# Linear attention feeding a two-layer MLP: fewer ones columns in the kv matmul, z spread in the mask multiply, one batch's num a slot later

## Chip, cores, metric

One core of one Trainium2 chip. The metric is device microseconds of the whole kernel. The inputs are fp32; the matmuls run in bf16 with fp32 sums.

## The reference, cut to what matters

```python
q_p, k_p = phi(q), phi(k)                          # phi(x) = elu(x) + 1; B=8, H=8, S=576, D=64
kv  = einsum('bhsd,bhse->bhde', k_p, v)
z   = sum(k_p, axis=2)
num = einsum('bhsd,bhde->bhse', q_p, kv)
den = einsum('bhsd,bhd->bhs', q_p, z)[..., None] + 1e-6
x   = (num / den)  ->  4608 tokens x 512
h   = x @ w_in                                     # 512 -> 2048
out = (h - tanh(h)) @ w_out                        # 2048 -> 512
```

## The kernel before

TensorE works through nine chunks of 512 tokens: 64 first-layer matmuls, then 64 of the second layer, each of 512 columns. The attention of the next batch is slipped into numbered slots between them (`s1[fi]` after a first-layer group, `s2[s]` after four second-layer matmuls). A batch has 576 tokens, so batch 2 is needed as chunk 2 starts.

```python
vp = const.tile([128, 2, J, 136], BF16, name="vp")     # J = 9; per row: 128 columns of v, 8 ones
...
def a_vp(b, i):                                         # VectorE copies v into vp
    nc.vector.tensor_copy(vp[:, i, :, 0:128].rearrange("p j (h d) -> p h j d", h=2), v_b[b % 2][:, 0:2, i])

def a_kv_cols(b, banks):                                # batches 2 to 7
    ...
    ps = [banks()[:, 0:272].rearrange("p (i e) -> p i e", i=2) for hg in range(2)]
    for i in range(2):
        for j in range(J):
            for hg in range(2):                         # two 64-row halves of the array: a pair
                r = slice(64 * hg, 64 * hg + 64)
                nc.tensor.matmul(ps[hg][:, i, :], kp[r, i, j].rearrange("p h d -> p (h d)"),
                                 vp[r, i, j, :], start=(j == 0), stop=(j == J - 1))
    for hg in range(2):
        nc.vector.tensor_mul(kz_t[b][:, hg, :, 0:136], ps[hg], mask[:, hg, :, 0:136])
...
# a_den:    four small matmuls per pair of heads with z, then rden = 1 / (den + 1e-6)
# a_spread: rden -> DRAM tile ds -> rdb, broadcast over 64 partitions (two DMA hops)
# a_num:    a 512-column matmul into PSUM bank 6 or 7, then xT = psum * rdb on VectorE
...
nc.gpsimd.memset(vp[:, :, :, 128:136], 1.0)
load_v(1)
load_wo(2)
load_wo(3)
...
    elif n1 < B:                                        # n1 = c + 1
        s1[8 if c == 1 else 5].append(lambda: a_kv_cols(n1, attn))
        s1[10 if c == 1 else 8].append(lambda: (a_den(n1, attn), a_spread(n1)))
        for p in range(NP + 1):                         # NP = 4: five nums
            s2[(11 if c == 1 else 9) + p].append(lambda p=p: a_num(n1, p))
```

The eight ones columns give z eight times over, so that one masked multiply puts z into the eight rows that den reads.

## Time and profile before

| | before |
|---|---|
| time, median of 3 runs | 294.0 us (293.95 to 294.2) |
| span of the profiled run | 291.8 us |
| TensorE / VectorE / ScalarE busy | 97% / 60% / 48% |
| kv block of one batch on TensorE | 1.17 us, six of them |
| chunks 3 to 6, each | 30.35 us |

A block's length is read from the start of its first matmul to the start of the next instruction's matmul, because the profile models the ends of matmuls. A chunk's length is read from the start of one chunk's first layer to the next one's in the chain of waits. Both are good to about 0.01 us.

### The profile page before, as it was taken

To read this page: it belongs to the slowest core of one execution; us is meant where nothing else is said; L and a number is where in the kernel's file an instruction comes from. 1 tells how busy PE (TensorE), PEld (TensorE's weight loads), DVE (VectorE), ACT (ScalarE), POOL (GpSimd) and SP (SyncE) were. 2 spreads that over 40 slices of the span, in tenths; PEclk is the share of its full clock that TensorE was granted. 3 is DMA by queue.
4 is the path that set the end of the run, shared out by engine and by line. 5 is a ranking of instruction groups with operands and counts; after the bars stand their busy time and mean duration, and the time that the engine had idled before them with its cause. 6 is when DMAs were issued, how large, how long until landed. Compare 5 with 4: busy or idle time off the path is not lost.

```text
span 291.8 us, 4476 instructions
## 1 busy us (share of the span) xinstructions
PE 284.2 (97%) x1775; PEld 134.5 (46%) x1803; DVE 174.8 (60%) x266; ACT 139.7 (48%) x168; POOL 33.1 (11%) x55
## 2 busy tenths in 40 slices
PE   8999999999999999999999999999999999999994
PEld 3544464454454444544444445444444444444443
DVE  4759958987458674776478637865581457106600
ACT  4838638846254733465345534751551155126411
POOL 8673030110030003000300030000000000000000
PEclk9999999999999999999999999999999999999999
DMA  6999999998989668955795579766117310130032
GB/s 96 198 204 212 208 207 213 214 168 145 253 158 159 170 131 135 200 139 127 134 223 131 120 137 196 144 142 139 32 34 168 73 36 0 42 84 20 0 74 72
DMA packets 39077, 38.94 MB, mean 133 GB/s; under 512 B 16336, under 2 KB 33808, under 8 KB 38288
## 3 DMA queue, kind: packets, MB, share of 16 engines
q0 software_dynamic: 17552, 18.35, 39.0%
q1 hardware_dynamic: 21344, 20.17, 30.5%
q8 instruction: 14, 0.23, 0.3%
q10 hardware_dynamic: 160, 0.13, 0.1%
q14 instruction: 7, 0.06, 0.1%
HBM read 43.91 MB, written 9.55 MB: 183 GB/s over the span
## 4 chain that ended last, share of the span: by engine, by line
PE 75%; DMA 18%; POOL 2%; issue 1%; SPq 1%; DVE 1%; ACT 1%; DVEq 0%; POOLq 0%
PE ps_all L366 37%; PE ps_all L387 32%; DMA w_out_sb<-in_moe_w_out_dram 6%; DMA w_in_sb<-in_moe_w_in_dram 3%; DMA rdb<-ds 3%; DMA out_dram<-osb 2%; PE ps_all L199 2%; DMA kraw<-in_k_dram 2%; PE ps_all L317 2%; DMA ds<-rden 1%; PE ps_all L276 1%; POOL v L419 1%; ACT osb L396 1%; SPq L401 0%; POOL qraw L90 0%
## 5 line engine op out<-in xcount | busy, mean ns | idle before, releaser
L366 PE MATMUL ps_all<-xT,w_in_sb 128*128 128x512 bf16 x558 | 126.5, 380 | 0.9 <-issue 0.2
L387 PE MATMUL ps_all<-w_out_sb,gT 128*128 128x512 bf16 x548 | 126.2, 380 | 0.7
L373 DVE TENSOR_TENSOR gT<-ps_all,th 128x1024 bf16<-128x1024 f32 x64 | 77.9, 1218 | 59.7 <-ACT th L372 59.7
L372 ACT ACTIVATE th<-ps_all 128x1024 f32<-128x1024 f32 x64 | 65.5, 1023 | 57.0 <-PE ps_all L366 46.4
L366 PEld LDWEIGHTS <-w_in_sb 128*128 128x128 bf16 x574 | 55.0, 98 | 66.0
L387 PEld LDWEIGHTS <-gT 128*128 128x128 bf16 x560 | 54.1, 98 | 64.7 <-issue 0.6
L396 ACT COPY osb<-ps_all 128x512 f32<-128x512 f32 (+1 forms) x36 | 20.8, 582 | 72.3 <-PE ps_all L387 55.9
L328 DVE TENSOR_TENSOR xT<-ps_all,rdb 128x512 bf16<-128x512 f32 x24 | 16.3, 689 | 13.7 <-PE ps_all L317 11.2
L134 ACT ACTIVATE e<-qraw 128x1152 bf16<-128x1152 bf16 x16 | 18.5, 1161 | 7.3 <-DMA qraw<-in_q_dram 7.3
L134 ACT ACTIVATE e<-kraw 128x1152 bf16<-128x1152 bf16 x15 | 17.4, 1162 | 0.1
L136 DVE TENSOR_TENSOR qp<-e,r 128x1152 bf16<-128x1152 bf16 x16 | 12.1, 758 | 7.8 <-ACT e L134 7.0
L136 DVE TENSOR_TENSOR kp<-e,r 128x1152 bf16<-128x1152 bf16 x15 | 11.4, 758 | 7.9 <-ACT e L134 7.0
L383 POOL COPY g<-qT 1x1 bf16<-1x1 bf16 x5 | 0.9, 182 | 119.7 <-DMA qT<-qp 119.7
L378 DVE TENSOR_TENSOR gT<-ps_all,th 128x512 bf16<-128x512 f32 x16 | 10.3, 686 | 2.3 <-ACT th L377 1.7
L377 ACT ACTIVATE th<-ps_all 128x512 f32<-128x512 f32 x16 | 9.2, 598 | 4.4 <-PE ps_all L366 3.2
L444 PE MATMUL ps_all<-zero 128*128 128x512 bf16 x29 | 9.3, 487 | 1.2 <-DVE zero L405 1.2
L317 PE MATMUL ps_all<-qT,kz 128*128 128x512 bf16 x28 | 10.1, 380 | 0.1
L135 DVE TENSOR_SCALAR r<-qraw 128x1152 bf16<-128x1152 bf16 x16 | 7.3, 453 | 1.9 <-DMA qraw<-in_q_dram 1.9
L199 PEld LDWEIGHTS <-kp 64*128 64x128 bf16 x216 | 6.4, 94 | 2.5 <-issue 2.5
L285 DVE RECIPROCAL rden<-den 128x144 f32<-128x144 f32 x7 | 7.4, 1052 | 0.2
L199 PE MATMUL ps_all<-vp,kp 64*128 64x136 bf16 x216 | 7.4, 220 | 0.0
L394 DVE COPY osb<-ps_all 128x128 f32<-128x128 f32 x1 | 0.3, 291 | 11.6 <-DMA out_dram<-osb 11.6
(84 smaller groups left out, 123.0 us busy)
## 6 DMA issues: line engine op xcount, KB each, us to landing
out_dram<-osb SPq DMA_DIRECT2D x70, 128.0 KB
rdb<-ds SPq DMA_DIRECT2D x12, 576.0 KB
kraw<-in_k_dram POOLq DMA_DIRECT2D x7, 576.0 KB, 7.1
qraw<-in_q_dram POOLq DMA_DIRECT2D x7, 576.0 KB, 9.2
v<-in_v_dram POOLq DMA_DIRECT2D x7, 576.0 KB, 11.9
w_out_sb<-in_moe_w_out_dram POOLq DMA_DIRECT2D x4, 512.0 KB, 16.0
w_in_sb<-in_moe_w_in_dram POOLq DMA_DIRECT2D x6, 256.0 KB, 8.6
qraw<-in_q_dram POOLq DMA_DIRECT2D x2, 288.0 KB, 4.4
```

What stands on the lines that cost most here:

```text
L134: return (lambda: nc.scalar.activation(e, x, AF.Exp), lambda: nc.vector.tensor_scalar(r, x, 0.0, 1.0, ALU.max, ALU.add), lambda: nc.vector ...
L136: lambda: nc.vector.tensor_tensor(y, e, r, ALU.min))
L199: nc.tensor.matmul(ps[hg][:, i, :], kp[r, i, j].rearrange("p h d -> p (h d)"), vp[r, i, j, :], start=(j == 0), stop=(j == J - 1))
L317: nc.tensor.matmul(ps, kz[:, p // 2, p % 2, 0:128], qT[:, p % 2, 0:8, p // 2, :], start=True, stop=True)
L328: nc.vector.tensor_mul(xT[:, p, S * b:S * b + 512].rearrange("p (j t c) -> p j t c", j=8, t=4), ps.rearrange("p j (t c) -> p j t c", t=4), ...
L366: nc.tensor.matmul(h, w_in_sb[:, 2 * (p % 2) + p // 2, fi * 128:(fi + 1) * 128], xT[:, p, c * 512:(c + 1) * 512], start=(n == 0), stop=(n ...
L372: nc.scalar.activation(th, h, AF.Tanh)
L373: nc.vector.tensor_sub(gT[:, fi:fi + 2, :], h, th)
L378: nc.vector.tensor_sub(gT[:, fi, :], h, th)
L387: nc.tensor.matmul(o, gT[:, fi, i * 128:(i + 1) * 128], w_out_sb[:, fi, :], start=(fi == 0), stop=(fi == NF - 1))
L396: nc.scalar.copy(osb[:, f0:f1], o[:, f0:f1])
L444: nc.tensor.matmul(ps_all[:, 0, :], zero[:, 0:128], zero, start=True, stop=True)
```

## The change

The intent is to stream six columns fewer in each of 216 kv matmuls, to make z's eight copies in the mask multiply instead, with a broadcast operand, and to ask for rdb later in the one batch where TensorE was seen waiting for it.

```diff
-    vp = const.tile([128, 2, J, 136], BF16, name="vp")
+    vp = const.tile([128, 2, J, 130], BF16, name="vp")
...
-        ps = [banks()[:, 0:272].rearrange("p (i e) -> p i e", i=2) for hg in range(2)]
+        ps = [banks()[:, 0:260].rearrange("p (i e) -> p i e", i=2) for hg in range(2)]
...
-            nc.vector.tensor_mul(kz_t[b][:, hg, :, 0:136], ps[hg], mask[:, hg, :, 0:136])
+            nc.vector.tensor_mul(kz_t[b][:, hg, :, 0:128], ps[hg][:, :, 0:128], mask[:, hg, :, 0:128])
+            nc.vector.tensor_mul(kz_t[b][:, hg, :, 128:136], ps[hg][:, :, 128:129].to_broadcast([128, 2, 8]),
+                                 mask[:, hg, :, 128:136])
...
-    nc.gpsimd.memset(vp[:, :, :, 128:136], 1.0)
+    nc.gpsimd.memset(vp[:, :, :, 128:130], 1.0)
...
-                s2[(11 if c == 1 else 9) + p].append(lambda p=p: a_num(n1, p))
+                s2[min(12 + p, 15) if c == 1 else 9 + p].append(lambda p=p: a_num(n1, p))
```

## The prediction

> **What bounds the kernel now.** I read the page's busy shares first, then the chain that ended last, then the timeline of the places that the diff touches.
>
> ```profile
> PE 284.2 (97%) x1775; PEld 134.5 (46%) x1803; DVE 174.8 (60%) x266; ACT 139.7 (48%) x168; POOL 33.1 (11%) x55
> ...
> PEclk9999999999999999999999999999999999999999
> ```
>
> TensorE is busy 97% of the 291.8 us span at full clock; VectorE (60%) and ScalarE (48%) have room. A change is worth what it does to the TensorE stream. The chain in order of time shows where that stream waits:
>
> ```profile
> 22.23 0.16 POOL vp L420
> 22.39 0.66 POOL v L93
> 23.05 17.84 DMA w_out_sb<-in_moe_w_out_dram
> 40.89 0.04 issue
> 40.93 0.38 PE ps_all L387
> ...
> 69.80 7.88 DMA rdb<-ds
> 77.71 0.05 DVEq L328
> 77.76 0.04 issue
> 77.80 0.70 DVE xT L328
> 78.50 0.04 issue
> 78.54 0.38 PE ps_all L317
> ```
>
> From 80.98 us to 278 us the chain is TensorE alone, and chunks 2 to 6 are all 30.35 us long. The tail shows output DMAs, but each ScalarE copy there starts as its own matmuls end (the second layer's groups come every 3.45 us), so I take TensorE to set it too. Of the change's three places, the kv block of one batch and the masked copy behind it look like this in the timelines of TensorE and VectorE:
>
> ```profile
> 58.06 1.24 PE L199 MATMUL ps_all<-vp,kp 64*128 64x136 bf16 x36
> 59.23 1.90 PE L366 MATMUL ps_all<-xT,w_in_sb 128*128 128x512 bf16 x7
> 61.06 0.43 PE L276 MATMUL ps_all<-qT,kz 128*32 128x144 bf16 x16
> ...
> 59.69 0.78 DVE L202 TENSOR_TENSOR kz<-ps_all,mask 128x272 bf16<-128x272 f32 x2
> 61.37 1.23 DVE L373 TENSOR_TENSOR gT<-ps_all,th 128x1024 bf16<-128x1024 f32 x1 [0.90 <-ACT th L372]
> ```
>
> The block occupies TensorE from 58.06 to 59.23, 1.17 us, six times in the kernel (7 us of 292). The third place is the num of batch 2, in chunk 1:
>
> ```profile
> 76.12 0.38 PE L317 MATMUL ps_all<-qT,kz 128*128 128x512 bf16 x1
> 77.20 0.38 PE L317 MATMUL ps_all<-qT,kz 128*128 128x512 bf16 x1
> 77.80 1.89 DVE L328 TENSOR_TENSOR xT<-ps_all,rdb 128x512 bf16<-128x512 f32 x3 [2.49 <-DMA rdb<-ds]
> 78.54 0.38 PE L317 MATMUL ps_all<-qT,kz 128*128 128x512 bf16 x1
> 79.62 0.38 PE L317 MATMUL ps_all<-qT,kz 128*128 128x512 bf16 x1
> 80.81 2.54 PE L366 MATMUL ps_all<-xT,w_in_sb 128*128 128x512 bf16 x11
> ```
>
> The nums come every 1.08 us (four second-layer matmuls and one num, 5 x 0.216), except the third: due at 77.20 + 1.08 = 78.28, it started at 78.54. Two PSUM banks alternate, the third num needs the first one's bank, and VectorE could not empty that before rdb landed. TensorE lost **0.26 us**. This wait is once only; in later batches the nums stand at slots 9 to 13, long after rdb.
>
> **What the Trainium skill says.** First, "TensorE: Matmul & The Clock Gate", section Back-to-back issue gap, gives N/2.4 + 2.5 ns per warm matmul, so time follows columns. The trace agrees: 136 columns would be 59.2 ns, and I derive 58.3 ns per pair below. Second, "TensorEngine Tiling (Array Packing)", Key Properties, says that different tiles run in parallel and that a change of tiling mode drains the engine. The trace agrees: two 64-row matmuls share one pitch, and the last kv start is 0.15 us before the full-height matmul that follows; that part does not shrink. Third, "VectorE: DVE Perf Modes", The TRN2 errata, has (N+151)/0.96 ns for an fp32 tensor_tensor, so a tiny one is nearly all fixed cost: 174 ns for 16 elements. The trace agrees nearly: 168 ns for 8 elements, 216 ns for 64 from PSUM (L214). Fourth, "Advanced Engine Details and Errata", SBUF Cachelines, gives lines of 16 bytes and a penalty where accesses change line too often. A row of vp goes from 272 bytes (17 lines) to 260, so most rows start off a line; no streamed row of this kernel does so now, so no trace settles that.
>
> **The change, part by part.**
>
> *Fewer columns.* The pitch of a kv pair from this trace: the 36 matmuls span 1.24 us with the last one's 0.220 us, so 35 steps take 1.02 us: 29.1 ns each, 58.3 ns per pair. Likewise batch 1's block with 192 columns (L177: 36 in 1.66 us, 0.243 each) gives 81.0 ns per pair, and batch 0's with 128 (L221: 18 in 0.68 us, 0.217 each) 54.5 ns. So (81.0 - 54.5)/64 = 0.414 ns per column. Six columns off: 2.5 ns per pair x 18 pairs = 45 ns per batch, 1.17 us becoming 1.125; x 6 batches = **0.27 us**, all on TensorE's path.
>
> *The mask multiply in two.* Each 272-element multiply (430 ns) becomes one of 256 (424 ns, L225's row of the same form) and one of 16. The 16-element one: L214's 216 ns less 48 elements at 1.04 ns = 166 ns. VectorE gains 12 x (424 + 166 - 430) = 1.9 us of busy time. On the clock less: consecutive VectorE instructions start about 80 ns before the end of the one ahead (the two of 430 ns lie 350 ns apart), so kz is whole 0.16 us later per batch. Does anything wait for it? In chunk 1 kz is complete at 60.47, den starts at 61.06; in chunk 2, 89.17 and 89.96. Slacks of 0.59 and 0.79 us take 0.16. The next VectorE work behind it idled 0.90 and 1.09 us for ScalarE. So **0**.
>
> *Num of batch 2 one slot later.* A slot is 0.86 us of second-layer matmuls. The first num starts at 76.98, the second at 78.06, the third at 79.14, when the first bank has been free since 78.50: the 0.26 us wait goes. But the slots are now 12, 13, 14, 15, 15: the fourth and the fifth num stand in the last slot, and chunk 2 follows at once. Call the third num's start T = 79.14. The fourth starts at T + 1.08; VectorE starts 0.42 us after a num's start (79.62 to 80.04), takes 0.69 us, and TensorE follows 0.04 us later, so xT of p = 3 is usable at T + 1.08 + 0.42 + 0.69 + 0.04 = T + 2.23. The vp copy ahead of it on VectorE is no obstacle (T + 1.02, next start 0.38 later, before T + 1.50). TensorE: fourth num 0.216, four small matmuls of the fifth 0.11 (80.70 to 80.81 now), three matmuls of chunk 2 0.65: it wants p = 3 at T + 2.05. So a **new wait of 0.18 us** takes the place of the old one. The fifth num's bank is no problem: the third's is emptied at T + 1.11, wanted at T + 1.30. Net: p = 3 of chunk 2's first group starts at 79.14 + 2.23 = 81.37 instead of 81.46, so only **0.09 us** is left.
>
> *Smaller memset.* GpSimd's L420 falls from 144 elements to 36; slope (1077 - 237)/(1152 - 144) = 0.83 ns, so 237 becomes 147 ns, and the two loads behind it start 0.09 us sooner. The transposes at 40.20 should hand over near 40.70 (nine took 0.50 at 9.24 to 9.74), and the second layer starts at 40.93, when the w_out piece has landed: a wait of some 0.2 us. But that piece took 17.84 us in a queue that was always full, so I expect bandwidth and not issue to set it: **0.03 us**, a guess between 0 and 0.09.
>
> Sum: 0.27 + 0.09 + 0.03 = 0.39 us; 294.0 - 0.4 = **293.6 us**.
>
> **Rivals.** *(A) Weight loads bind, not columns.* Then fewer columns give nothing: 293.9. For it: weight loads are busy 1.06 us of the 1.17. Against it: the ones matmul of batch 0 (L210) loads the same kp form with 32 columns, 18 in 0.39 us, 0.174 each, 25 ns per pair. I give it 7%. *(B) Rows off the 16-byte line slow the moving stream or the copy into vp.* A pitch 10% longer would cost 0.6 us (294.2), half rate 6 us (300). Nothing in the trace speaks for it, nothing excludes it: 8%. *(C) The VectorE work becomes a wait* (den before kz). It would have to use up 0.59 us; 3%, and it would add some 0.1 us a batch. *(D) The new wait at chunk 2's start does not occur*, since my 0.18 is a difference of modelled steps: then the whole 0.26 stays and the time is 293.4. 20%. *(E) The new wait is larger than the old one*, with a late rdb or VectorE late by one instruction: 293.8. 15%.
>
> **Range and chances.** The parts lie between 0 and -0.65 us together, and the three runs of before spread over 0.25 us. That gives 293.15 to 294.15, with the prediction a little below the middle and rival B's tail outside. No mechanism here is worth 5.9 us in the good direction, since the whole kv work is 7 us and waits on TensorE's path are some 0.5 us: faster 0.005. Slower by 2% needs B at half rate: 0.015. Within 2%: 0.98.
>
> **What would show each step right or wrong.** The kv block should read 130 columns and last 1.12 to 1.13 us to the next first-layer matmul; 1.17 means A, more means B. The masked multiplies should show 12 of 256 elements at 424 ns and 12 of 16 at about 166, with no TensorE wait behind kz. The nums of batch 2 should all lie 1.08 us apart, with no hole before the third, and the fourth first-layer matmul of chunk 2 should start about 0.18 us late; no hole there means D. Chunks 2 to 6 should be 30.30 us each. The memset should be near 150 ns and the handover at 40.93 hardly earlier. A chunk longer than 30.35, or a change of the total beyond 1 us, would prove the account wrong.

## The result, and the profile after

| | before | after |
|---|---|---|
| time, median of 5 runs | 294.1 us (293.95 to 294.2) | 293.99 us (293.48 to 294.38) |
| ratio | | 0.9994, 95% interval 0.998 to 1.0009 |
| span of the profiled run | 291.8 us | 292.2 us |
| kv block | 1.17 us | 1.15 to 1.16 us |
| chunks 3 to 6, each | 30.35 us | 30.34 us |

A ratio is the mean time of one kernel's runs over that of the other's runs of the same rounds, so it is not quite the ratio of the medians quoted. Executions over 1.5% slower than the fastest of the same kernel are left out of the means. The kernel is as fast as before within what the runs resolve.

The busy line of the changed kernel's page, answering to the first line of the prediction:

```profile
PE 285.0 (98%) x1803; PEld 134.2 (46%) x1803; DVE 176.0 (60%) x278; ACT 139.7 (48%) x168; POOL 32.9 (11%) x55
```

Twelve VectorE instructions more (266 to 278) and 1.2 us more of VectorE time; TensorE is the bound as before. (The counts of TensorE differ because some matmul records were missing from the trace of before, 1775 against 1803.)

The kv block of batch 2 and the mask multiplies behind it, in the timelines of TensorE and VectorE of the changed kernel (start, length, engine, line, operation):

```profile
58.64 1.22 PE L199 MATMUL ps_all<-vp,kp 64*128 64x130 bf16 x36
59.80 1.90 PE L368 MATMUL ps_all<-xT,w_in_sb 128*128 128x512 bf16 x8
61.63 0.43 PE L278 MATMUL ps_all<-qT,kz 128*32 128x144 bf16 x16
...
60.59 0.17 DVE L203 TENSOR_TENSOR kz<-ps_all,mask 128x16 bf16<-128x16 f32 x1
60.67 0.42 DVE L202 TENSOR_TENSOR kz<-ps_all,mask 128x256 bf16<-128x256 f32 x1
61.00 0.17 DVE L203 TENSOR_TENSOR kz<-ps_all,mask 128x16 bf16<-128x16 f32 x1
```

The block is 59.80 - 58.64 = 1.16 us long, where 1.125 was predicted. kz is whole at 61.00 + 0.17 = 61.17, and den starts at 61.63, so nothing waits for the second multiply.

The nums of batch 2 and the start of chunk 2 in the changed kernel's timeline:

```profile
77.54 0.38 PE L319 MATMUL ps_all<-qT,kz 128*128 128x512 bf16 x1
78.38 1.36 DVE L330 TENSOR_TENSOR xT<-ps_all,rdb 128x512 bf16<-128x512 f32 x2 [2.51 <-DMA rdb<-ds]
78.62 0.38 PE L319 MATMUL ps_all<-qT,kz 128*128 128x512 bf16 x1
79.70 0.38 PE L319 MATMUL ps_all<-qT,kz 128*128 128x512 bf16 x1
80.78 0.38 PE L319 MATMUL ps_all<-qT,kz 128*128 128x512 bf16 x1
81.11 3.15 PE L368 MATMUL ps_all<-xT,w_in_sb 128*128 128x512 bf16 x13
81.20 0.69 DVE L330 TENSOR_TENSOR xT<-ps_all,rdb 128x512 bf16<-128x512 f32 x1
81.94 2.04 PEld L368 LDWEIGHTS <-w_in_sb 128*128 128x128 bf16 x10 [0.30 <-issue]
```

The nums are evenly 1.08 us apart: the hole before the third is gone. But the fourth num's multiply ends at 81.20 + 0.69 = 81.89, and chunk 2's fourth matmul, due at 81.11 + 3 x 0.216 = 81.76, goes at 81.94. A hole of 0.18 us has taken its place. The trip of rden to rdb has left the chain of waits altogether.

The opening of the changed kernel's profiled run, which outweighs all of this (timeline of TensorE):

```profile
39.02 1.66 PE L177 MATMUL ps_all<-v,kp 64*128 64x192 bf16 x36 [0.25 <-DMA v<-in_v_dram]
...
41.52 1.02 PE L389 MATMUL ps_all<-w_out_sb,gT 128*128 128x512 bf16 x4 [0.22 <-DMA w_out_sb<-in_moe_w_out_dram]
```

The second layer's first matmul after batch 1's transposes was at 40.93 us before and is at 41.52 us here, 0.59 us later. That is why the profiled span grew, although everything behind it became shorter.

To keep the opening out, I compare from here on what I call the **body**: from that matmul to the first second-layer matmul of the last chunk. Both starts are read from the timeline of TensorE. The body was 274.03 - 40.93 = 233.10 us before and is 274.43 - 41.52 = 232.91 us after.

### The profile page after: what moved, and what is told of

Read it like the earlier page. It is cut to its first block, busy times and chain, and to the rows that moved or that the text cites. A ratio compares the mean times of both kernels' runs of the same rounds, so it can differ in the third digit from the quotient of the medians.

```text
span 292.2 us, 4516 instructions
## 1 busy us (share of the span) xinstructions
PE 285.0 (98%) x1803; PEld 134.2 (46%) x1803; DVE 176.0 (60%) x278; ACT 139.7 (48%) x168; POOL 32.9 (11%) x55
## 4 chain that ended last, share of the span: by engine, by line
PE 81%; DMA 14%; POOL 2%; ACT 1%; issue 1%; SPq 0%; DVE 0%; POOLq 0%
PE ps_all L368 38%; PE ps_all L389 37%; DMA w_out_sb<-in_moe_w_out_dram 6%; DMA w_in_sb<-in_moe_w_in_dram 3%; DMA out_dram<-osb 2%; DMA kraw<-in_k_dram 2%; PE ps_all L199 2%; PE ps_all L319 2%; PE ps_all L278 1%; POOL v L421 1%; ACT osb L398 1%; SPq L403 0%; POOL qraw L90 0%; PE ps_all L322 0%; POOL qraw L93 0%
## 5 line engine op out<-in xcount | busy, mean ns | idle before, releaser
L389 PE MATMUL ps_all<-w_out_sb,gT 128*128 128x512 bf16 x560 | 127.5, 379 | 0.2 <-DMA w_out_sb<-in_moe_w_out_dram 0.2
L375 DVE TENSOR_TENSOR gT<-ps_all,th 128x1024 bf16<-128x1024 f32 x64 | 77.9, 1219 | 58.3 <-ACT th L374 58.3
L446 PE MATMUL ps_all<-zero 128*128 128x512 bf16 x29 | 8.4, 445 | 1.2 <-DVE zero L407 1.2
L199 PE MATMUL ps_all<-vp,kp 64*128 64x130 bf16 x216 | 7.3, 217 | 0.0
```

The source lines that it names most:

```text
L375: nc.vector.tensor_sub(gT[:, fi:fi + 2, :], h, th)
L389: nc.tensor.matmul(o, gT[:, fi, i * 128:(i + 1) * 128], w_out_sb[:, fi, :], start=(fi == 0), stop=(fi == NF - 1))
```

## The experiments

My theory after the result: the six columns are worth the predicted 45 ns a batch, but rows 260 bytes apart take two thirds of that back; the slot shift swaps one wait for another of like size; and the opening's spread hides what is left. The rivals: the kv pitch has a floor that columns do not lower; the second mask multiply costs time somewhere; the change itself delays the opening. Eleven runs were made, two of them of unedited kernels. All gave correct results, and each stood beside runs of the kernel before on the same chip; three of them (264-byte rows, the kernel before again, 272-byte rows in the old slots) are single executions, whose times are not compared.

### Rows of 272 bytes, 130 columns read

```diff
-    vp = const.tile([128, 2, J, 130], BF16, name="vp")
+    vp = const.tile([128, 2, J, 136], BF16, name="vp")
-                                     vp[r, i, j, :], start=(j == 0), stop=(j == J - 1))
+                                     vp[r, i, j, 0:130], start=(j == 0), stop=(j == J - 1))
```

> The changed kernel with the rows of vp 272 bytes apart again, of which the matmuls still read 130 columns. Theory 'rows off the 16-byte line' (each streamed row of 260 bytes starts off a 16-byte line and that costs what the six columns save): the pair pitch in the kv block falls from 57.9 ns to 55.3-55.8 ns, the block from 1.155 to about 1.12 us, chunks 3 to 6 from 30.34 to 30.30-30.31 us. Rival 'a floor' (the pitch at this size is set by something that columns do not change, the weight loads or the issue): the pitch stays at 57.9 ns and the chunks at 30.34 us. Time either way within 0.3 us of the changed kernel, so the verdict comes from the profile.

Measured: median 293.61 us, ratio to before 0.9986 (0.9974 to 0.9998). The chain's first-layer pieces at the starts of chunks 4 and 5, of the kernel before, the changed kernel and this one:

```profile
141.69 5.18 PE ps_all L366 x24
172.04 5.18 PE ps_all L366 x24
```

```profile
142.13 5.18 PE ps_all L368 x24
172.47 5.18 PE ps_all L368 x24
```

```profile
141.84 5.18 PE ps_all L368 x24
172.15 5.18 PE ps_all L368 x24
```

The chunks are 30.35, 30.34 and 30.31 us (three in a row give 30.355, 30.340 and 30.310 on average). The kv block is 1.13 us (86.33 to 87.46 in this run's timeline). By the prediction's own working, the 36 matmuls span 1.19 us with the last one's 0.217, so a pair takes (1.19 - 0.217)/35 x 2 = 55.6 ns; with 260-byte rows the same working gives 57.9 ns ((1.23 - 0.217)/35 x 2, batch 3). Both are good to about 0.6 ns, since the spans are printed to 0.01 us; the chunk lengths put the difference at (30.340 - 30.310)/18 = 1.7 ns per pair. So there is no floor at the pitch of the changed kernel, and the columns are worth what was predicted: 0.04 us per block and chunk. The PSUM side is the same in both kernels, so it is the rows of vp. The multiply in two pieces is in here too, and costs nothing.

### Rows of 264 bytes

```diff
-    vp = const.tile([128, 2, J, 130], BF16, name="vp")
+    vp = const.tile([128, 2, J, 132], BF16, name="vp")
-                                     vp[r, i, j, :], start=(j == 0), stop=(j == J - 1))
+                                     vp[r, i, j, 0:130], start=(j == 0), stop=(j == J - 1))
```

> The changed kernel with the rows of vp 264 bytes apart (every row on 8 bytes, every other one on 16), 130 columns read. If what costs is a row's start off a 16-byte line, half the rows cost and the kv block lies between 1.13 and 1.155 us, about 1.14; if 4 bytes off an 8-byte boundary is what costs, the block is 1.13 us as with 272 bytes; if it must be 16 or nothing and the cost is per pair of rows, 1.155 us.

Measured (one run, 293.51 us, state unknown, so its pitches are used and not its time): five of the six blocks are 1.14 us by the timeline, one 1.15, and three chunks, from 111.36 to 202.34 us in the chain, take 30.33 us each. It lies in between, as it should when every other row is off a 16-byte line. If vp itself starts on such a line, 13 of the 18 rows of a partition are off one with 260 bytes, 9 with 264 and none with 272. Against 272-byte rows the chunks are 0.030 us longer with 260 bytes and 0.017 us with 264 (30.340 and 30.327 less 30.310), which is 2.3 and 1.9 ns lost per row that is off. So the count of rows fits roughly, with about 2 ns each; that 16 bytes are the line is argued from these three pitches. An 8-byte boundary as the whole cause is excluded, since 264-byte rows all lie on one. A rival is not tested: a narrower vp can also move the tiles that are allocated behind it. The weight loads of kp took 94 ns on average at all three pitches, which speaks against it for that tile.

### The slot shift alone, and the columns alone

```diff
# shift alone, in the kernel before
-                s2[(11 if c == 1 else 9) + p].append(lambda p=p: a_num(n1, p))
+                s2[min(12 + p, 15) if c == 1 else 9 + p].append(lambda p=p: a_num(n1, p))
# columns alone, in the changed kernel: the same line turned back
```

> The kernel before with only the num of batch 2 one slot later. Theory: the hole of 0.26 us before the third num goes and one of 0.17-0.18 us comes before the fourth matmul of chunk 2, so 0.09 us is left; chunks 3 to 6 stay at 30.35 us; ratio 0.9997. Rival: the new hole belongs to the two-piece mask multiply or the 260-byte rows, then it is absent here and the gain is 0.26 us, ratio 0.9991.

> The changed kernel with the num of batch 2 in its old slots. Theory: the hole of about 0.26 us before the third num is there as in the kernel before, no hole at chunk 2's start, chunks 30.34 us; over the six kv blocks 0.09 us gained, ratio about 0.9997 (a tie). Rival: the two-piece multiply or the narrower rows cost time somewhere (den waiting for kz, the copy into vp): then a chunk is longer than 30.35 us and the ratio is above 1. The opening up to the second half of batch 1's transposes will show whether its 0.6 us of delay in the changed kernel's profile comes with the columns (again near 41.5 us) or is run to run (near 40.9 us).

Measured: shift alone 293.96 us, ratio 0.9998 (0.9986 to 1.001); columns alone 293.69 us, ratio 0.9989 (0.9977 to 1.0002). With the shift alone, chunk 2 starts at 81.00 us, and its fourth matmul, due at 81.65, goes at 81.83: the hole of 0.18 us belongs to the shift. Its body is 233.00 us.

The columns alone gave the surprise. The expected hole of 0.26 us before the third num was **not there**, although the nums stand in their old slots (timeline of the columns-only run):

```profile
76.54 0.38 PE L319 MATMUL ps_all<-qT,kz 128*128 128x512 bf16 x1
77.62 0.38 PE L319 MATMUL ps_all<-qT,kz 128*128 128x512 bf16 x1
77.86 1.94 DVE L330 TENSOR_TENSOR xT<-ps_all,rdb 128x512 bf16<-128x512 f32 x3 [2.14 <-DMA rdb<-ds]
78.70 0.38 PE L319 MATMUL ps_all<-qT,kz 128*128 128x512 bf16 x1
```

The third num is on time. From the end of rden to VectorE's first multiply took 13.55 us here (64.31 to 77.86), and 13.91 us in the profile of before (63.89 to 77.80). A hole of 0.26 at 13.91 puts the point where TensorE starts to wait at 13.65 us, and 13.55 is below it. (In the profile of before the third num is due 78.28 - 63.89 = 14.39 us after the end of rden, and it goes 78.54 - 77.80 = 0.74 us after VectorE's first multiply begins: 14.39 - 0.74 = 13.65.)

### The kernel before once more, and 272-byte rows with the old slots

> The kernel before, unedited, for a second profile. If the wait before the third num of batch 2 is set by the trip of rden through memory to rdb: hole = trip (end of rden to VectorE's first num) less 13.65 us, no hole below that (13.91 gave 0.26, the columns-only run's 13.55 gave none). If it belongs to the kernel before as such, 0.26 us again whatever the trip. The opening between 40.9 and 41.5 us.

> Rows of 272 bytes with 130 columns read, num of batch 2 in its old slots: a third point for the same rule, hole before the third num = trip less 13.65 us, and no hole in chunk 2; kv blocks 1.13 us, chunks 3 to 6 30.31 us.

One profile each (293.5 and 293.57 us, state unknown; used for their waits). The second profile of the kernel before, timeline:

```profile
77.28 0.38 PE L317 MATMUL ps_all<-qT,kz 128*128 128x512 bf16 x1
77.70 1.89 DVE L328 TENSOR_TENSOR xT<-ps_all,rdb 128x512 bf16<-128x512 f32 x3 [2.31 <-PE ps_all L317]
78.45 0.38 PE L317 MATMUL ps_all<-qT,kz 128*128 128x512 bf16 x1
```

| old slots | rden's trip to rdb | trip - 13.65 | hole before third num |
|---|---|---|---|
| before, first profile | 13.91 us | 0.26 | 0.26 us (sets the rule) |
| before, second profile | 13.73 us | 0.08 | 0.09 us |
| 272-byte rows, old slots | 13.68 us | 0.03 | 0.03 us |
| columns alone | 13.55 us | none | none |

(The second: rden ends at 62.92 + 1.05 = 63.97, VectorE starts at 77.70; the third num, due at 77.28 + 1.08 = 78.36, starts at 78.45. The profile puts VectorE's wait in this run down to TensorE's second num. But by the packed trace the second half of rdb landed at 77.58, 0.12 us before VectorE began, just as in the first profile, 77.68 and 77.80; so here too it waited for rdb.) The hole follows the trip. The same program had 0.26 us in one execution and 0.09 in another. So the wait that the shift was made for is worth 0 to 0.3 us depending on how two DMA hops went, while the new one is 0.18 us in all six profiles with the changed slots (the changed kernel twice, shift alone, 272- and 264-byte rows, late memsets). As an estimate, the rule put to the trips of all twelve profiles, 13.55 to 13.95 us, gives the old slots a hole of 0.13 us on average, so the shift as it was made costs slightly more than it saves.

### The changed kernel once more

> The changed kernel once more, unedited, on the chip of the three runs beside it. If the opening's delay is run to run, the second layer's first matmul after batch 1's transposes lies between 40.9 and 41.5 us (40.93 in the profile of before, 41.52 in that of the changed kernel, 41.39 in the shift-only run whose opening is the same program as before's). The hole before chunk 2's fourth matmul should be 0.17-0.18 us again, whatever the trip of rden through memory to rdb takes (13.5 to 14 us so far), kv blocks 1.15-1.16 us. Ratio to before 0.998 to 1.001.

Measured: 293.81 us, ratio 0.9996 (0.9984 to 1.0009). Hole in chunk 2: 0.18 us; blocks 1.15 to 1.16; body 274.44 - 41.52 = 232.92 us. The pitches and waits repeat to 0.01 us.

### Nums in slots 12, 13, 14, 14, 15

```diff
-                s2[min(12 + p, 15) if c == 1 else 9 + p].append(lambda p=p: a_num(n1, p))
+                s2[(12, 13, 14, 14, 15)[p] if c == 1 else 9 + p].append(lambda p=p: a_num(n1, p))
```

> The changed kernel with the nums of batch 2 in slots 12, 13, 14, 14, 15 in place of 12, 13, 14, 15, 15: the fourth follows the third at once. Theory: neither hole is left; xT of p = 3 is ready about 1.75 us after the third num's start and wanted 2.05 us after it, so chunk 2 starts its fourth matmul on time and the whole is 0.17-0.18 us shorter than the changed kernel from the third num on. Rival: the wait only moves, because the fourth num waits for its PSUM bank or VectorE has the copy into vp ahead of it; then a hole of 0.1 us or more shows before the fourth num, the fifth num or in chunk 2's first group.

Measured: 293.71 us, ratio 0.9991 (0.9979 to 1.0003), body 232.74 us, 0.17 us below the changed kernel's. Its timeline:

```profile
79.50 0.59 PE L319 MATMUL ps_all<-qT,kz 128*128 128x512 bf16 x2
80.80 0.28 PE L322 MATMUL ps_all<-qT,kz 128*128 128x64 bf16 x4
80.92 3.40 PE L368 MATMUL ps_all<-xT,w_in_sb 128*128 128x512 bf16 x15
```

The third and fourth num go back to back at 79.50, and 15 matmuls of chunk 2 take 3.40 us = 14 x 0.216 + 0.38: no hole. Its trip was 13.67 us, so rdb's delay was not put to a hard test here. It was below, at 13.82 us.

### Memsets behind the loads

```diff
-    for i in (1, 0):
-        nc.gpsimd.memset(v_b[i][:, 2], 1.0)
-    nc.gpsimd.memset(vp[:, :, :, 128:130], 1.0)
     load_v(1)
     load_wo(2)
     load_wo(3)
+    for i in (1, 0):
+        nc.gpsimd.memset(v_b[i][:, 2], 1.0)
+    nc.gpsimd.memset(vp[:, :, :, 128:130], 1.0)
```

> The changed kernel with the three memsets of ones behind the loads of v(1) and the last two pieces of w_out on GpSimd's queue, so that these loads are issued some 2.2 us sooner. Theory of the prediction (the queue is full, bandwidth sets the landing): the second layer still waits for w_out and starts at 41.2 to 41.5 us. Rival (issue sets it): both waits of about 0.25 us (v, then w_out) are gone, the start is at about 40.7 us and the kernel 0.3 to 0.7 us shorter than the changed one.

Measured: 293.69 us, ratio 0.9994 (0.9981 to 1.0008). GpSimd's and TensorE's timelines:

```profile
21.06 0.74 POOL L93 DMA_DIRECT2D v<-in_v_dram  x1 [0.53 <-DMA w_in_sb<-in_moe_w_in_dram]
22.34 0.74 POOL L115 DMA_DIRECT2D w_out_sb<-in_moe_w_out_dram  x1 [0.54 <-DMA w_in_sb<-in_moe_w_in_dram]
...
41.80 1.02 PE L389 MATMUL ps_all<-w_out_sb,gT 128*128 128x512 bf16 x4 [0.25 <-DMA w_out_sb<-in_moe_w_out_dram]
```

The v load is issued at 21.06 us in place of 22.62 in the changed kernel, and the w_out piece at 22.34 in place of 23.35. Before each issue GpSimd now waits about 0.5 us that the profile puts down to earlier transfers. The data come no sooner: the second layer still waits, until 41.80, later than the 41.2 to 41.5 expected. So the rival did not come true, and the prediction's view that bandwidth sets the landing fits; but this is one profile, and the opening varies by as much from run to run (see below).

### All three together, and without the memsets

The edits are the 272-byte rows, the slots 12, 13, 14, 14, 15 and, in the first of the two runs, the late memsets.

> Rows of 272 bytes with 130 columns read, nums of batch 2 in slots 12, 13, 14, 14, 15, memsets late. From the second layer's start after batch 1's transposes to the end it should be 0.5 us shorter than the kernel before's 250.87 us (six kv blocks of 1.13 in place of 1.17, and no hole before the third num nor in chunk 2), 250.35 to 250.45; the opening as in the memset run. Ratio to before 0.9965 to 0.9985. Rival: the sum of the parts is lost again in the opening's spread, then the ratio is not distinguishable from the 0.9986 of the 272-byte rows alone.

> Rows of 272 bytes with 130 columns read and nums of batch 2 in slots 12, 13, 14, 14, 15, memsets where the changed kernel has them. One of five executions of the run with all parts took 769.5 us with every 512-column matmul at about 0.6 us; if that came of the program, it should come again here (two of its three parts); if it was the chip, all executions here lie near 293.5 us. From the second layer's start after batch 1's transposes to the end 250.35 to 250.45 us (before 250.87, changed 250.68), kv blocks 1.13, no hole. Ratio to before 0.997 to 0.9995, median 293.4 to 293.7.

The first gave 293.26, 293.47, 293.49 and 293.54 us in four executions, ratio 0.9983 (0.9969 to 0.9997), and **769.5 us** in one, which was the profiled one. Its groups of lines:

```profile
L368 PE MATMUL ps_all<-xT,w_in_sb 128*128 128x512 bf16 x574 | 344.7, 832 | 0.0
L368 PEld LDWEIGHTS <-w_in_sb 128*128 128x128 bf16 x574 | 97.9, 173 | 231.5 <-issue 231.5
```

A 512-column matmul of the first layer took 344.7/574 = 0.60 us of TensorE's time on average instead of 0.216, while VectorE and ScalarE took nearly as long per instruction as ever (busy 179.9 and 140.8 us, against 176.0 and 139.7 in the changed kernel). The run lists a clock of 1.0, but its page has no PEclk row, so a lower clock is not excluded. I do not explain a slow execution by the kernel; its profile is not used, and what it was stays open.

Without the memsets all five executions were normal: 293.51 us (293.46 to 293.82), ratio 0.9988 (0.9975 to 1.0002). Body 274.21 - 41.64 = 232.57 us, blocks 1.13, from the second layer's start to the end 292.0 - 41.64 = 250.36 us as expected, and no hole at either place with a trip of 13.82 us, which would have cost 0.17 us in the old slots.

### The sum of the parts

The kernel before without its hole would have a body of 233.10 - 0.26 = 232.84 us. From there the parts add up: the kv gain of six blocks (0.015 us each with 260-byte rows, 0.028 with 264, 0.045 with 272, from the chunk lengths), the old hole of that run, and the new hole.

| run | kv | old hole | new hole | sum | body measured |
|---|---|---|---|---|---|
| before, second profile | 0 | +0.09 | 0 | 232.93 | 232.90 |
| changed kernel | -0.09 | 0 | +0.18 | 232.93 | 232.91 |
| shift alone | 0 | 0 | +0.18 | 233.02 | 233.00 |
| columns alone | -0.09 | none | 0 | 232.75 | 232.73 |
| slots 12, 13, 14, 14, 15 | -0.09 | 0 | 0 | 232.75 | 232.74 |
| 264-byte rows | -0.17 | 0 | +0.18 | 232.85 | 232.84 |
| 272-byte rows | -0.27 | 0 | +0.18 | 232.75 | 232.74 |
| 272-byte rows, old slots | -0.27 | +0.03 | 0 | 232.60 | 232.59 |
| 272-byte rows, slots 12, 13, 14, 14, 15 | -0.27 | 0 | 0 | 232.57 | 232.57 |

The account closes to 0.03 us. The starting matmul of the body, however, lay anywhere from 40.93 to 41.80 us. It was at 40.93, 41.03 and 41.39 in the three profiles whose opening is the program of before, and from 41.10 to 41.80 in the nine others. So 0.46 us of it is run to run with the same program. Whether the narrower vp also shifts the opening by a few tenths, by other addresses or a shorter memset, these runs cannot tell.

## Why the prediction was right, and where it was off

The time lies in the range (293.99 in 293.15 to 294.15), but 0.4 us above the point. That proves little: the range also holds the time of the kernel before (294.0 and 294.1), and the 95% interval of the ratio holds both no change and the 0.4 us that were forecast. The steps have to be judged from the traces:

- **TensorE as the bound: right.** Every gain and loss on its stream shows in the body to 0.03 us.
- **Fewer columns, 0.27 us: mis-sized.** It measured 6 x 0.015 = 0.09 us. The slope of 0.414 ns per column was right: with rows 272 bytes apart the same 130 columns give 0.27 us. What failed is that the sum took rows of 260 bytes to stream like those of 272. The prediction named this as rival B and gave it 8%; it came in a milder form than the 10% of pitch used there (1.7 ns of about 56, 3%), and it ate two thirds of the gain. Its other half, a slower copy into vp, did not show (452 ns on average in the columns-only run, 451 before). Rival A (weight loads bind) fell with the 272-byte rows.
- **Mask multiply in two: right.** 166 ns predicted and measured for the 16-element multiply, 416 against 424 ns for the other, and nothing waits for kz, so rival C fell too. (The prediction's 174 ns for 16 elements, like its 59.2 ns for 136 columns, is an estimate worked out from the formula of the page that it names; the traces show 166 and 58.3 ns.)
- **The new wait of 0.18 us at chunk 2's start: right,** to 0.01 us, in all six profiles with those slots, so rival D (it does not occur) fell. But the prediction forgot it when it wrote down its signs: the hole lies inside chunk 2, which took 30.52 us in the changed kernel (81.11 to 111.63), not the 30.30 named there, and by the letter a chunk longer than 30.35 us was to prove the account wrong. Chunks 3 to 6 are 30.34 us. Rival E (larger than the old one) did not come by the ways it named, but it holds wherever the trip is short, because the old wait is then smaller.
- **The old wait of 0.26 us: right for that profile, wrong as a property of the kernel.** It depends on the trip through memory, and was 0.26, 0.09, 0.03 and 0 us in four profiles with the old slots. So the shift's net is not 0.09 us gained: by the rule, it gains 0.08 us at a trip of 13.91 us and loses 0.18 us at 13.65 and below. That the first profile of before agreed with the forecast net was luck: its trip of 13.91 us lies near the long end of the 13.55 to 13.95 seen.
- **The memset: its length right, its worth not seen.** 149 ns against 147 predicted. With the memsets moved, an earlier issue brought the w_out piece no sooner in the one profile taken. The 0.03 us themselves are far below the spread of the opening.
- **The opening's spread: not allowed for.** The prediction treated the 40.93 us of one profile as fixed. The same program gave up to 41.39, which is as much as the whole predicted gain.

The best version found is the one with 272-byte rows and slots 12, 13, 14, 14, 15: on the body 0.53 us below the first profile of before and 0.34 us below the changed kernel, though its total, 0.9988 of before, does not stand clear of 1 in five runs.

## What to carry to other kernels

When a tile is narrowed to stream fewer columns, keep the row pitch where it was and read less of each row: a pitch that puts rows off a 16-byte line took back two thirds of the gain here. Before moving work to dodge a wait on a DMA trip, profile the unchanged kernel more than once, and work out what the new place makes wait: here a wait of 0 to 0.3 us was bought off with a fixed one of 0.18 us, and moving only one of the five pieces differently avoided both. Where gains are tenths of a microsecond, compare a stretch of the trace that starts behind the loads, because the opening's spread is larger than they are.

## What the Trainium skill lacked or had wrong

- "TensorE: Matmul & The Clock Gate", Back-to-back issue gap: the formula that the prediction took, N/2.4 + 2.5 ns, stands there for an isolated matmul, and for a stream of weight loads and matmuls the page has about 131 ns at 512 columns. Here 512-column matmuls with a weight load each followed one another every 216 ns, as by the formula. Neither figure takes in where a streamed row starts: 130 columns took 1.7 ns more per pair with rows 260 bytes apart than with rows 272 bytes apart.
- "Advanced Engine Details and Errata", SBUF Cachelines, gives the 16-byte line without a size for the penalty and does not say whether it holds for TensorE's streamed operand. The three pitches (260, 264, 272 bytes: chunks of 30.340, 30.327 and 30.310 us) agree roughly with a 16-byte boundary and give about 2 ns per row that starts off it.
- No page that I found gives the spread of a round trip through memory: the same two hops, rden to rdb, took 13.55 to 13.95 us in these runs, which decides whether TensorE waits.
- "TensorE: Matmul & The Clock Gate", Part 1, has a half-rate clock when cold and a 13/16 one under a current limit, and mentions a gate stuck at a quarter; as estimates from the 0.216 us here, these would make 512 columns 0.43, 0.27 and 0.86 us. One execution took 0.60 us per matmul on average, and by the packed trace most of its first-layer matmuls began 0.62 or 0.48 us after the one before, which none of the three gives by itself.
